# One DMA for the load of x and one for each tile's store, inverse stage 2 in half groups over two PSUM buffers, and layer norms sooner, in a long-convolution and MLP kernel

## The chip, the cores and the metric

The kernel runs on one core of one Trainium2 chip. The metric is the device time of one execution in microseconds (us), as the median of several executions; the kernel before took 240.22 us (three executions, 240.03 to 240.64). "Profile" and "trace" mean one execution recorded by the hardware profiler; its span is some 2 us shorter than the time (238.6 against 240.35 in the profiled execution), so spans are compared with spans and times with times. An execution counts as slow when it took over 1.5% more than the fastest of its kernel. Medians and ranges below are over all executions, slow ones too; ratios are of fast executions alone, and so are the profiles unless said otherwise.

In the views PE is TensorE (matmuls), DVE is VectorE, ACT is ScalarE, POOL is GpSimd, and SP is the engine that issues most DMAs; PSUM is the memory that matmuls write. The tiles: `pz` is what inverse stage 2 leaves in PSUM and `zt` its copy; `qln` and `hln` are the two layer norms, `pt` and `hlnT` the transposed `hln`; `ps1m` and `ps2m` are the two MLP layers' products, and `o` is a finished tile. The "granted clock" is the share of TensorE's full clock that it was given.

## The reference, cut to what matters

```python
# B, S, D, Dff = 1, 2048, 512, 1376; all inputs bfloat16
x  = A_q
q  = layernorm(x)
kv = shift_conv(A_k, A_shift_k) * A_v
y  = irfft(rfft(pad(kv)) * rfft(pad(A_ssm_k)))[:S] + kv * A_ssm_D   # long convolution over S
h  = x + q * y
out = h + relu(layernorm(h) @ B_w1) @ B_w2
```

The kernel computes the convolution as a Fourier transform in two stages of matmuls each way. The change is in what follows: the last inverse stage ("inverse stage 2"), the two layer norms and the start of the MLP.

## The kernel before

The 2048 tokens are 16 row tiles of 128 rows, in four groups of four tiles. `xh` holds x for all tiles, later h. A tile's token order is permuted: partition 32a + b of tile t holds token 64b + 16a + t, so a tile is four pieces of 32 rows in DRAM.

```python
def _tokens(src2d, t0, nt):            # four access patterns of 32 rows each
    D = src2d.shape[1]
    return [bass.AP(tensor=src2d.tensor, offset=src2d.offset + (16 * a + t0) * D, ap=[[64 * D, 32], [1, nt * D]])
            for a in range(4)]
# ...
for a, src in enumerate(_tokens(x_d, 0, NT)):
    nc.sync.dma_start(out=xh[32 * a:32 * a + 32, :, :].rearrange("p t d -> p (t d)"), in_=src)
# ... loads of w1 and w2 on the same queue
pzp = pl.push("psZ", bufs=1, space=PSUM)      # 4 banks, one buffer
ptp = pl.push("psT", bufs=1, space=PSUM)      # 1 bank, for the transposes
psum = pl.push("psM", bufs=3, space=PSUM)     # 3 banks, for the MLP

def inv2(q):                                  # inverse stage 2 of a group: small fp32 matmuls
    pz = pzp.tile([P, 4, 4, P], F32, tag="pz", name="pz")
    # ... 32 matmuls of 32x32 by 128 columns for each tile (two records each in a trace)
    return pz

def inv2_copy(q, pz):                         # four ACT copies pz -> zt, one for a tile
    # ...

def chain(q):                                 # groups 1 to 3: off the critical path, transposed by DMA
    qln = ln1(q)                              # layer norm of x
    hln = new_rows(q)
    gate(q, four(q), qln, hln)                # h = x + qln * z, then the layer norm of h
    # ... dma_start_transpose hln -> hlnT

# in mlp2(sc), for each tile: o = ps2 + xh, then
for a, dst in enumerate(_tokens(out_d, t, 1)):
    nc.sync.dma_start(out=dst, in_=o[32 * a:32 * a + 32, :])

# the schedule
qln = ln1(0, on_act=True)
inv2_copy(0, inv2(0))
hln = new_rows(0)
gate(0, [0, 1], qln, hln, on_act=True)
gate(0, [2, 3], qln, hln, on_act=True)
pz = inv2(1)
transposes(0, hln)                            # 8 TensorE transposes and one ACT copy to hlnT
mlp1(0, slice(0, 2 * P))                      # MLP layer 1 for the first two tiles
transposes(2, hln)
inv2_copy(1, pz)
mlp1(0, slice(2 * P, 4 * P))
chain(1)
inv2_copy(2, inv2(2))
mlp2(0)
chain(2)
mlp1(1)
# ... inv2(3), mlp2(1), chain(3), then mlp1 and mlp2 of groups 2 and 3
```

## Time and profile before

| what | before, us | from |
|---|---|---|
| time | 240.22 | median of 3 |
| span of the profile | 238.6 | profile |
| xh's DMAs issued from | 107.25 | timeline |
| DVE first reads xh | 124.19 | timeline |
| first matmul of inverse stage 2 | 124.99 | chain |
| first MLP matmul | 141.08 | chain |
| first matmul of inverse stage 2 of group 2 | 154.90 | timeline |
| last residual add (o) done | 234.77 | timeline |

The rows are the milestones used below. The views themselves stand in the prediction. In a chain each line is the start, the length, and what the end of the kernel hung on in that stretch.

### The profile page before, as it was taken

What the parts mean: (1) busy time and instruction counts of PE and PEld (TensorE: products, weight loads), DVE (VectorE), ACT (ScalarE), POOL (GpSimd) and SP (SyncE); (2) the same over time, 40 slices, a digit from 0 to 9 for tenths busy, and PEclk for the clock granted to TensorE, in tenths of its full rate; (3) what the DMA queues carried; (4) which work ended last, traced back from release to release, by engine and by line L of the source; (5) the groups of instructions that cost most, each with busy time, mean ns of one, the idle gap of its engine ahead of it and who ended that gap; (6) DMA issues with size and microseconds to landing.
All of it is one profiled execution on the core that took longest, in us unless ns stands there. A gap on an engine that the chain in (4) does not pass through costs nothing.

```text
span 238.6 us, 7218 instructions
## 1 busy us (share of the span) xinstructions
PE 206.1 (86%) x3100; PEld 145.8 (61%) x3100; DVE 154.2 (65%) x299; ACT 130.7 (55%) x241; POOL 62.7 (26%) x88
## 2 busy tenths in 40 slices
PE   0486998999767999998989678899999999979992
PEld 0473555999646999978986546764446444434440
DVE  7886986877655989977995882822577257740031
ACT  3779464666775688897992338912262327105500
POOL 6399700000003999975000001020022002200000
PEclk9999999999955899999999779999999999999998
DMA  6999910000000000009992000023200420042011
GB/s 212 286 206 157 190 34 4 3 1 0 3 5 3 3 1 0 3 1 201 195 368 70 3 3 0 3 46 69 61 8 3 93 71 17 0 91 65 23 44 44
DMA packets 30191, 15.45 MB, mean 65 GB/s; under 512 B 25584, under 2 KB 29008, under 8 KB 30032
## 3 DMA queue, kind: packets, MB, share of 16 engines
q1 hardware_dynamic: 29088, 14.93, 28.3%
q8 instruction: 24, 0.39, 0.7%
q10 hardware_dynamic: 1072, 0.07, 0.4%
q14 instruction: 7, 0.06, 0.1%
HBM read 7.08 MB, written 2.10 MB: 38 GB/s over the span
## 4 chain that ended last, share of the span: by engine, by line
PE 79%; ACT 9%; DMA 5%; DVE 4%; issue 2%; SPq 0%; ACTq 0%
PE ps1m L486 16%; PE ps2m L496 15%; PE pz L417 9%; PE psi L389 6%; PE pst L196 5%; PE psy L326 5%; PE pkv L254 5%; PE u L226 4%; PE u L228 4%; DMA sk<-in_A_ssm_k_dram 4%; PE ps L212 3%; PE ps2k L226 3%; PE ps2k L228 3%; ACT zt L425 2%; ACT c2c L174 2%
## 5 line engine op out<-in xcount | busy, mean ns | idle before, releaser
L488 ACT ACTIVATE h1T<-ps1m 128x512 bf16<-128x512 f32 (+3 forms) x55 | 28.0, 515 | 39.3 <-PE ps1m L486 38.5
L486 PE MATMUL ps1m<-hlnT,w 128*128 128x512 bf16 (+3 forms) x220 | 40.5, 346 | 4.5 <-ACT hlnT L508 2.2
L496 PE MATMUL ps2m<-w,h1T 128*128 128x512 bf16 (+1 forms) x176 | 38.7, 379 | 0.0
L486 PEld LDWEIGHTS <-w 128*128 128x128 bf16 (+1 forms) x220 | 22.6, 103 | 22.1 <-issue 5.3
L499 DVE TENSOR_TENSOR o<-ps2m,xh 128x512 bf16<-128x512 f32 x16 | 11.0, 691 | 38.2 <-PE ps2m L496 38.2
L316 DVE TENSOR_TENSOR t<-u,kf 128x704 fp32r<-128x704 f32 x32 | 27.1, 889 | 4.8 <-ACT usb L312 4.8
L496 PEld LDWEIGHTS <-h1T 128*128 128x128 bf16 (+1 forms) x176 | 17.0, 98 | 21.1 <-issue 0.8
L316 POOL TENSOR_TENSOR t<-usb,kf 128x320 fp32r<-128x320 f32 x32 | 28.7, 924 | 3.4 <-ACT usb L312 2.3
L417 PE MATMUL pz<-bp,ecore 32*32 32x128 f32 x1024 | 22.1, 387 | 4.2 <-ACT zt L425 2.2
L434 POOL TENSOR_SCALAR rstd<-mv 128x4 f32<-128x4 f32 x6 | 1.4, 229 | 88.5 <-DVE mv L441 88.5
L417 PEld LDWEIGHTS pz<-bp,ecore 32*32 32x32 f32 x1024 | 15.8, 108 | 9.8 <-issue 2.9
L439 DVE BATCH_NORM_STATS2 st<-xh 128x6 f32<-128x512 bf16 x32 | 19.8, 680 | 0.0
L328 ACT CAST kf<-psy 128x512 fp32r<-128x512 f32 x32 | 18.4, 645 | 1.6
L389 PE MATMUL psi<-dre,kf 128*128 128x256 f32 x64 | 15.8, 288 | 0.9 <-ACT kf L328 0.9
L425 ACT CAST zt<-pz 128x512 bf16<-128x512 f32 x16 | 8.2, 602 | 13.9 <-PE pz L417 13.9
L326 PE MATMUL psy<-t,ipos 128*128 128x512 f32 x48 | 15.8, 390 | 0.0
L389 PE MATMUL psi<-dim,kf 128*128 128x256 f32 x64 | 15.4, 283 | 0.0
L254 PE MATMUL pkv<-kT,wdiag 128*128 128x512 bf16 x64 | 15.2, 381 | 0.0
L196 PE MATMUL pst<-ident,sk 128*128 128x128 bf16 x64 | 6.7, 299 | 9.2 <-DMA sk<-in_A_ssm_k_dram 9.2
L201 ACT CAST a1k<-ps 128x512 fp32r<-128x512 f32 x20 | 10.4, 593 | 6.7 <-PE ps L212 6.7
L283 DVE TENSOR_TENSOR kf<-ps2k,dtab 128x512 fp32r<-128x512 f32 x16 | 11.0, 694 | 3.5 <-PE ps2k L228 3.4
L284 ACT CAST kf<-ps2k 128x512 fp32r<-128x512 f32 x16 | 10.2, 641 | 5.5 <-PE ps2k L228 5.3
(108 smaller groups left out, 410.0 us busy)
## 6 DMA issues: line engine op xcount, KB each, us to landing
sk<-in_A_ssm_k_dram SPq DMA_DIRECT2D x1, 2048.0 KB, 8.4
xh<-in_A_q_dram SPq DMA_DIRECT2D x4, 512.0 KB, 8.6
out_dram<-o SPq DMA_DIRECT2D x64, 32.0 KB, 1.6
w<-in_B_w_dram SPq DMA_DIRECT2D x1, 1376.0 KB, 15.1
w<-in_B_w_dram SPq DMA_DIRECT2D x1, 1280.0 KB, 18.2
hlnT<-hln SPq DMA_TRANSPOSE x12, 2.5
w<-in_B_w_dram SPq DMA_DIRECT2D x1, 96.0 KB, 17.8
dtab<-in_A_ssm_D_dram ACTq DMA_DIRECT2D x2, 32.0 KB, 8.4
```

Source lines behind the costliest of these rows:

```text
L196: nc.tensor.transpose(out=pst[:, i, :], in_=src[:, :, :, 8 * q + i], identity=ident[:])
L226: nc.tensor.matmul(out=ps[:, kk, :], lhsT=w_re[:, k1, :], rhs=a_in[:, k1, :], start=True, stop=False, skip_group_check=True)
L254: nc.tensor.matmul(out=ps[:], lhsT=wdiag[:, rg, j, :], rhs=kT[c][:, rg, 16 - j:CH + 16 - j], start=(j == 0), stop=(j == KS - 1))
L316: eng.tensor_tensor(out=t[:, :, j, :], in0=in0.unsqueeze(1).to_broadcast([P, 2, n, 2]), in1=kfr[:, :, j, ks], op=ALU.mult)
L326: nc.tensor.matmul(out=psy[:], lhsT=m_[:], rhs=t_.rearrange("p j k -> p (j k)"), start=first, stop=not first)
L328: nc.scalar.copy(out=kf[:, s, :, 2 * kp:2 * kp + 2], in_=psy[:].rearrange("p (j k) -> p j k", k=2))
L389: nc.tensor.matmul(out=ps[:, i, :], lhsT=kf[:, c, 4 * m:4 * m + 4, :].rearrange("p r k -> p (r k)"), rhs=d[:].rearrange("p a b -> p (a b)" ...
L417: nc.tensor.matmul(out=pz[32 * a:32 * a + 32, r4, l4, :], lhsT=ecore[rows, rho, n2, :], rhs=rhs, start=(rho == 0), stop=(rho == 1), tile_p ...
L439: nc.vector.bn_stats(out=st[:, t % 4, :], in_=xh[:, t, :])
L486: nc.tensor.matmul(out=ps1[:fsz, :], lhsT=w1[:, c, fc * P:fc * P + fsz], rhs=hlnTs[sc][:, c, part], start=(c == 0), stop=(c == DC - 1))
L488: nc.scalar.activation(out=h1s[sc][:fsz, fc, part], in_=ps1[:fsz, :], func=ACT.Relu)
L496: nc.tensor.matmul(out=ps2[:], lhsT=h1s[sc][:ksz, fc, i * P:(i + 1) * P], rhs=w2[:ksz, fc, :], start=(fc == 0), stop=(fc == NFC - 1))
```

## The change

The intent has four parts. Two PSUM buffers of four banks each, of which each half of a group takes one, so that group 1 of inverse stage 2 needn't wait for all of group 0's copies (half groups). The second eight transposes midway through the first MLP pass (midway transposes). The first layer norm of groups 2 and 3 ahead of the MLP layer that precedes them on DVE (layer norms sooner). And one DMA for four (xh's load and each tile's store).

```diff
 def _tokens(src2d, t0, nt):
-    return [bass.AP(..., offset=src2d.offset + (16 * a + t0) * D, ap=[[64 * D, 32], [1, nt * D]])
-            for a in range(4)]
+    return bass.AP(..., offset=src2d.offset + t0 * D, ap=[[16 * D, 4], [64 * D, 32], [1, nt * D]])
@@ load of xh
-    for a, src in enumerate(_tokens(x_d, 0, NT)):
-        nc.sync.dma_start(out=xh[32 * a:32 * a + 32, :, :].rearrange("p t d -> p (t d)"), in_=src)
+    nc.sync.dma_start(out=xh[:].rearrange("p t d -> p (t d)"), in_=_tokens(x_d, 0, NT))
@@ pools
-    pzp = pl.push("psZ", bufs=1, space=PSUM)
-    ptp = pl.push("psT", bufs=1, space=PSUM)
-    psum = pl.push("psM", bufs=3, space=PSUM)
+    pzp = pl.push("psZ0", bufs=2, space=PSUM)
@@ store of a tile
-            for a, dst in enumerate(_tokens(out_d, t, 1)):
-                nc.sync.dma_start(out=dst, in_=o[32 * a:32 * a + 32, :])
+            nc.sync.dma_start(out=_tokens(out_d, t, 1), in_=o[:])
@@ schedule
-    inv2_copy(0, inv2(0))
     hln = new_rows(0)
-    gate(0, [0, 1], qln, hln, on_act=True)
-    gate(0, [2, 3], qln, hln, on_act=True)
-    pz = inv2(1)
+    for ts in ([0, 1], [2, 3]):
+        inv2_copy(0, ts)                      # inv2 of half a group, then its two copies
+        gate(0, ts, qln, hln, on_act=True)
+    for ts in ([0, 1], [2, 3]):
+        inv2_copy(1, ts)
+    pl.pop("psZ0")
+    ptp = pl.push("psT", bufs=1, space=PSUM)
+    psum = pl.push("psM", bufs=3, space=PSUM)
+    pzp = pl.push("psZ", bufs=1, space=PSUM)
     transposes(0, hln)
-    mlp1(0, slice(0, 2 * P))
-    transposes(2, hln)
-    inv2_copy(1, pz)
+    mlp1(0, slice(0, 2 * P), lambda: transposes(2, hln))
     mlp1(0, slice(2 * P, 4 * P))
-    chain(1)
-    inv2_copy(2, inv2(2))
+    chain(1, ln1(1))
+    inv2_copy(2)
+    qln = ln1(2)
     mlp2(0)
-    chain(2)
+    chain(2, qln)
 # ... group 3 likewise
```

More of the change, by code (lines that the diff above doesn't have):

```diff
@@ L51, in _tokens @@
     D = src2d.shape[1]
-    return [bass.AP(tensor=src2d.tensor, offset=src2d.offset + (16 * a + t0) * D, ap=[[64 * D, 32], [1, nt * D]])
-            for a in range(4)]
+    return bass.AP(tensor=src2d.tensor, offset=src2d.offset + t0 * D, ap=[[16 * D, 4], [64 * D, 32], [1, nt * D]])
 @with_exitstack
@@ L406, with inv2 @@
     zts, hlnTs, h1s = {}, {}, {}
-    def inv2(q):
+    def inv2(q, l4s=(0, 1, 2, 3)):
         pz = pzp.tile([P, 4, 4, P], F32, tag="pz", name="pz")
-        for l4 in range(4):
+        for l4 in l4s:
             for rho in range(2):
@@ L420, in inv2, with inv2_copy @@
         return pz
-    def inv2_copy(q, pz):
-        zts[q] = hp.tile([P, 4, D], BF16, tag="zt", name="zt")
-        for l4 in range(4):
+    def inv2_copy(q, l4s=(0, 1, 2, 3)):
+        pz = inv2(q, l4s)
+        if q not in zts:
+            zts[q] = hp.tile([P, 4, D], BF16, tag="zt", name="zt")
+        for l4 in l4s:
             nc.scalar.copy(out=zts[q][:, l4, :].rearrange("p (m r) -> p m r", r=4),
@@ L469, in new_rows, with chain @@
         return ep.tile([P, 4, D], BF16, tag="hln", name="hln")
-    def chain(q):
-        qln = ln1(q)
+    def chain(q, qln):
         hln = new_rows(q)
@@ L476, in chain, with mlp1 @@
             nc.sync.dma_start_transpose(out=hlnTs[q][:, :, i * P:(i + 1) * P], in_=hln[:, i, :])
-    def mlp1(sc, part=slice(0, 512)):
+    def mlp1(sc, part=slice(0, 512), midway=None):
         if sc not in h1s:
@@ L482, in mlp1 @@
         for fc in range(NFC):
+            if fc == NFC // 2 and midway is not None:
+                midway()
             fsz = min(P, DFF - fc * P)
@@ L510 @@
     qln = ln1(0, on_act=True)
-    inv2_copy(0, inv2(0))
     hln = new_rows(0)
-    gate(0, [0, 1], qln, hln, on_act=True)
-    gate(0, [2, 3], qln, hln, on_act=True)
-    pz = inv2(1)
+    for ts in ([0, 1], [2, 3]):
[7 more added lines that the diff above has]
+    pzp = pl.push("psZ", bufs=1, space=PSUM)
     transposes(0, hln)
-    mlp1(0, slice(0, 2 * P))
-    transposes(2, hln)
-    inv2_copy(1, pz)
+    mlp1(0, slice(0, 2 * P), lambda: transposes(2, hln))
     mlp1(0, slice(2 * P, 4 * P))
-    chain(1)
-    inv2_copy(2, inv2(2))
+    chain(1, ln1(1))
+    inv2_copy(2)
+    qln = ln1(2)
     mlp2(0)
-    chain(2)
+    chain(2, qln)
     mlp1(1)
-    inv2_copy(3, inv2(3))
+    inv2_copy(3)
+    qln = ln1(3)
     mlp2(1)
-    chain(3)
+    chain(3, qln)
     for sc in (2, 3):
```

## The prediction

In it, k is the number of DMA engines that one DMA uses. Engines are out of step when a piece of 16 KB takes them 0.629 us, the fastest of the kernel before, and in step when it takes 1.28 us, the steady state there.

> **What bounds the kernel now.** I read the busy shares first, then the chain of work that ended last, then the timeline from 117 us, the waits of TensorE and the DMA table.
>
> ```profile
> PE 206.1 (86%) x3100; PEld 145.8 (61%) x3100; DVE 154.2 (65%) x299; ACT 130.7 (55%) x241; POOL 62.7 (26%) x88
> ...
> PEclk9999999999955899999999779999999999999998
> ```
>
> TensorE is busy 86% of the span and carries 79% of the chain. The second row is its granted clock in slices of 6 us; the dip to 7 lies at 131 to 143 us, in the part that the change rebuilds. Everything before 124 us is untouched. From there the chain reads (start, length, what):
>
> ```profile
> 124.99 4.42 PE pz L417 x188
> 129.41 0.51 issue
> 129.92 1.31 PE pz L417 x44
> 131.31 2.06 ACT zt L425 x4
> 133.42 4.58 PE pz L417 x188
> ...
> 139.43 0.57 PE pt L507 x8
> 140.02 1.02 ACT hlnT L508
> 141.08 6.44 PE ps1m L486 x44
> 147.52 0.46 PE pt L507 x8
> 148.00 1.01 ACT hlnT L508
> 149.01 1.96 ACT zt L425 x4
> 150.97 0.30 ACT h1T L488
> 151.31 3.65 PE ps1m L486 x32
> ...
> 211.04 0.70 DVE o L499
> 211.75 0.45 SPq L476
> 212.29 2.45 DMA hlnT<-hln
> ```
>
> The reader sees the places where the chain leaves TensorE: the four zt copies at 131.31 (one pz buffer of four PSUM banks, so group 1 waits for group 0's copies), the two hlnT copies, the zt copies at 149.01 that sit in ACT's queue ahead of the Relu copies, and the last hln transposes. TensorE's own waits there are 2.20 us at 131.2, 1.10 at 140, 1.10 at 148, 0.78 at 150.5 and 1.49 at 213.4. The rest after 154.90 is matmul upon matmul (the chain has stretches of 9.5 to 9.7 us of one MLP stage each), which the change doesn't touch.
>
> The last view is the DMA table (KB of each, us from issue to landing), with the first reader of xh in the timeline:
>
> ```profile
> sk<-in_A_ssm_k_dram SPq DMA_DIRECT2D x1, 2048.0 KB, 8.4
> xh<-in_A_q_dram SPq DMA_DIRECT2D x4, 512.0 KB, 8.6
> out_dram<-o SPq DMA_DIRECT2D x64, 32.0 KB, 1.6
> ```
>
> ```profile
> 124.19 2.46 DVE L439 BATCH_NORM_STATS2 st<-xh 128x6 f32<-128x512 bf16 x4
> ```
>
> xh is issued from 107.25; its fourth part is issued at 108.6 and lands 11.5 later, at 120.1. DVE first reads it at 124.19, so today there are 4.1 us of slack and nobody waits for it.
>
> [...] Before, a part has 32 rows on both sides: k = 16. Afterwards the DRAM side is [4, 32, row], and the built program carries it so, beside 128 partitions: k = 4. No DMA of the kernel before has such a shape, so its trace can't confirm it. [...] in the transfer records a 16 KB piece of xh took 0.629 us at its fastest (26 GB/s) but 1.28 us in the steady state, where 16 engines write 32 partitions; all of xh moved in 10.9 us, 192 GB/s. [...] the clock was 0.50 at 134 to 136 us and at 142 to 144, after the gaps at 131 and 140. [...]
>
> **The change part by part, first with xh in time.**
>
> *Half groups.* A half is 64 of 128 matmuls, about 2.7 us at the rate of 124.99 to 129.41. Group 0 ends at 131.2 as now, but its first half is out at 127.7, is copied (two copies of 0.51) by 128.8, and the gate of the first two tiles starts when qln is ready, 128.98 (now 131.93). Group 1 follows without the 2.20 us wait and ends near 137.2 instead of 139.4. The gate takes 4.3 us a half as now (first qln product 131.93 to last hln 136.22), so the second hln half is done near 137.5 (now 140.3). But ACT runs in order: the copies of group 1 stand behind the square root of the second gate half (136.5), and the transposes' bank is one of group 1's, free at 137.5. Then 0.57 transposes, 1.0 hlnT copy behind the last zt copies (138.6): the first MLP matmul starts at 139.7 instead of 141.08, 1.4 us sooner.
>
> *Midway transposes.* The second 8 transposes run between matmuls and their copy beside them. Gone: 1.10 + 0.78. The 88 matmuls of 128x256 took 0.146 us each in the first pass (half of it at the low clock) and 0.1195 in the second; if the low-clock stretches go, another 1.2. From 139.7: 88 x 0.1195 + 0.5 = 11.0, plus 0 to 1.5 for a low clock, ends at 150.7 to 152.2 (now 154.90). Gain 2.7 to 4.2, including the 1.4.
>
> *Layer norms sooner.* ln1 of group 3 (2.46 + 0.36 + 1.5 POOL + 1.38 = 5.7 us) moves ahead of mlp2(1), so its gate starts at about 195.1 instead of 200.5, and the transposes end 5 us sooner. The wait of 1.49 goes. The other groups have slack of over 5 us: 0.
>
> *One DMA for a tile.* SP issues 4 x 0.42 us now; the last of the kernel starts at 236.1, 1.3 after o is done (234.77). With 16 engines this would save about 0.9. With 4, each engine has 32 rows of 1 KB at 0.048 us (the trace's median) = 1.5 us[...]: 0.4 to 1.9 lost.
>
> Sum with xh in time: -2.7 to -4.2, -1.5, and at the end -0.9 to +1.5: about -5, 235 us.
>
> **The xh load.** With k = 4 each engine moves 32 rows of 16 KB. Estimate from the trace's durations: first piece 1.8 us after issue, at 109.0; 32 x 0.629 = 20.1 us, landing at 129; [...] 32 x 1.28 = 41 us, landing at 150. Call the landing L. From L: stats to qln 4.8 us (124.19 to 128.98 now), the first gate half to L + 9.1, second to L + 13.5, because it needs zt copies that stand behind the first square root on ACT; group 1's copies follow the second root, L + 14.5; hlnT copy L + 15.5; MLP from L + 15.6, 12.5 us with one cold window, ends at L + 28.1. Against 154.90 that is L - 126.8: +2.7 us for L = 129.5, +23 for 150. Taking off 1.5 for the last chain and adding about 1 at the end: +2 (242) or +22 (262). In the early case the half groups just pay for the late xh. w1 and w2 queue behind xh on those engines, but by 4 x 8 x 0.113 = 3.6 us and some 4 more only, before their readers.
>
> **Rivals.**
> - k is 16 after all (the lowering reshapes the pattern): [...] xh at least as early as now, and the gain of 5 us stands: 233.5 to 235.5. For it: sk, 128 rows in one DMA, moves 2 MB in 8.4 us. [...]
> - k = 4, the engines drift out of step: 242. For: some first pieces of xh in the records started 0.4 to 0.7 us after the others. [...]
> - k = 4 in step: 262. [...] Against: whoever wrote the change would have seen so large a loss, if it was timed.
> - The MLP's PSUM buffers bind (ACT's 1.0 us copy midway delays three buffers of 0.59 each): at most 0.5 us.
> - A lower clock eats the gain: 1.5 us.
>
> **Range and chances.** I give the in-time case 0.3 (its gain of 2.0 to 2.8% straddles the line, two thirds of it over 2%), 242 a weight of 0.35 and the slow case with what lies between 0.35. The middle of that is 243; eight in ten lie within 234 to 263. Faster by over 2%: 0.20; within: 0.43; slower: 0.37.
>
> **What would show it.** xh's single DMA: landing 20 us or 40 us after issue says k = 4, 6 to 11 says 16. If late, DVE's first stats start after 124.2 with a wait on the DMA, and ACT's zt copies wait for the square root. The pz group 1 should begin at once after group 0 if xh is in time. The chain should show no zt copies at 149, no DMA hlnT at 212. out DMAs should land in 2.5 us or more if k = 4. I am wrong altogether if xh lands late and the time still falls, or if it lands early and the time doesn't.

## The result, and the profile after

The changed kernel took 263.79 us (median of four, 263.21 to 263.98), the kernel before 240.43 us in the same rounds (240.03 to 243.92). The ratio is 1.0974, 95% interval 1.0946 to 1.1002: slower by 9.7%. A ratio here is the mean time of one kernel's fast runs over that of the other's of the same rounds, so it is not quite the ratio of the medians quoted.

First the page of the changed kernel, TensorE's row of busy times and the granted clock in 40 slices (of 6.5 us here):

```profile
PE 206.3 (79%) x3085; PEld 147.3 (56%) x3100; DVE 154.1 (59%) x299; ACT 130.6 (50%) x241; POOL 62.4 (24%) x88
...
PEclk9999999999657999999995555599999999999997
```

TensorE's work is the same, 206.3 us against 206.1, in a span 23 us longer. The five slices at 5, from 137 to 170 us, cover most of the time in which it stood still, and its first work after that. Next the chain of waits of the same kernel:

```profile
109.25 40.51 DMA xh<-in_A_q_dram
...
149.78 2.47 DVE st L437 x4
...
161.41 0.29 ACT rstd L429
161.70 1.94 ACT zt L423 x4
...
163.69 1.02 PE pt L505 x8
...
165.85 4.42 PE ps1m L485 x20
```

The end of the kernel now hangs on the load of x for 40.5 us. From its landing at 149.75 the first gate runs, half by half, then group 1's copies (zt), the transposes (pt) and the MLP (ps1m) at 165.85, where before the MLP began at 141.08. DVE's first read of xh in the timeline carries the wait itself (start, length, and in brackets the idle time and its releaser):

```profile
149.78 2.47 DVE L437 BATCH_NORM_STATS2 st<-xh 128x6 f32<-128x512 bf16 x4 [23.49 <-DMA xh<-in_A_q_dram]
```

and the DMA table has one issue for each load and store:

```profile
xh<-in_A_q_dram SPq DMA_DIRECT2D x1, 2048.0 KB
out_dram<-o SPq DMA_DIRECT2D x16, 128.0 KB
```

Beneath these views lie the records of single transfers. The DMAs end with records of 4 bytes, read here as one for each engine that a DMA used. There were 1841 such records before and 821 after. Taking away 64 stores and 4 loads of 16 each and adding 17 DMAs of 4 each gives 1841 - 1088 + 68 = 821. Four transfers of 16 KB for xh were under way at once for 33.9 of its 38.5 us, where 16 were for 7.8 of 10.9 us before. And of the pieces of w1 and w2, which are issued behind xh, just a quarter (128 of 512 and 344 of 1376) started only from 147.4 us on; the last of them ended at 156.6. So the single load used four engines of 16. The 128 pieces of 16 KB that make up xh took 1.22 us each in the median, 0.608 at the fastest, and ran for 38.5 us together.

| distance, us | before | after |
|---|---|---|
| issue of xh to landing | 12.9 to the last part (107.25 to 120.1) | 40.5 |
| xh needed or landed to first MLP matmul | 16.9 (124.19 to 141.08) | 16.1 |
| first MLP matmul to group 2's inverse stage 2 | 13.8 | 12.6 |
| from there to the end of the span | 83.7 | 83.5 |

So the whole loss is the load. What the other three parts gave is only some 2 us in this table, and the question is whether the rest was hidden behind the late load or never there.

### The profile page after: what moved, and what is told of

Same layout as the page of the kernel before. It is cut to its first block, busy times and chain, and to the rows that moved or that the text cites. A ratio compares the mean times of both kernels' runs of the same rounds, so it can differ in the third digit from the quotient of the medians.

```text
span 261.9 us, 7138 instructions
## 1 busy us (share of the span) xinstructions
PE 206.3 (79%) x3085; PEld 147.3 (56%) x3100; DVE 154.1 (59%) x299; ACT 130.6 (50%) x241; POOL 62.4 (24%) x88
## 4 chain that ended last, share of the span: by engine, by line
PE 64%; DMA 19%; DVE 7%; ACT 5%; issue 3%; POOLq 0%; DVEq 0%; ACTq 0%
DMA xh<-in_A_q_dram 15%; PE ps1m L485 15%; PE ps2m L495 15%; PE psy L325 6%; PE pst L195 5%; PE pkv L253 4%; PE pz L413 4%; PE u L225 4%; PE u L227 3%; DMA sk<-in_A_ssm_k_dram 3%; PE ps L211 3%; PE ps2k L227 3%; PE ps2k L225 3%; DVE st L437 2%; ACT c2c L173 2%
## 5 line engine op out<-in xcount | busy, mean ns | idle before, releaser
L495 PE MATMUL ps2m<-w,h1T 128*128 128x512 bf16 (+1 forms) x172 | 38.5, 379 | 0.2
L429 ACT ACTIVATE rstd<-mv,eps_t 128x2 f32<-128x2 f32 (+1 forms) x3 | 0.9, 296 | 30.7 <-DVE mv L439 30.7
L387 PE MATMUL psi<-dim,kf 128*128 128x256 f32 x64 | 15.4, 283 | 0.0
L200 ACT CAST a1k<-ps 128x512 fp32r<-128x512 f32 x20 | 10.4, 594 | 8.3 <-PE ps L211 8.3
L387 PEld LDWEIGHTS psi<-dre,kf 128*128 128x128 f32 x64 | 12.2, 191 | 1.6 <-ACT kf L327 1.3
```

The costliest lines, as they stand in the source:

```text
L387: nc.tensor.matmul(out=ps[:, i, :], lhsT=kf[:, c, 4 * m:4 * m + 4, :].rearrange("p r k -> p (r k)"), rhs=d[:].rearrange("p a b -> p (a b)" ...
L495: nc.tensor.matmul(out=ps2[:], lhsT=h1s[sc][:ksz, fc, i * P:(i + 1) * P], rhs=w2[:ksz, fc, :], start=(fc == 0), stop=(fc == NFC - 1))
```

## The experiments

Eleven runs of ten kernels, all correct. The first four undo or isolate the DMAs.

### xh4: the changed kernel with xh loaded in four DMAs again

```diff
-    nc.sync.dma_start(out=xh[:].rearrange("p t d -> p (t d)"), in_=_tokens(x_d, 0, NT))
+    for a, src in enumerate(_tokens4(x_d, 0, NT)):      # the old four patterns
+        nc.sync.dma_start(out=xh[32 * a:32 * a + 32, :, :].rearrange("p t d -> p (t d)"), in_=src)
```

> The changed kernel with the row load xh in its four old DMAs again (k = 16 engines each); half groups, sooner layer norms and the single store of each tile stay. Theory A (the single xh load on 4 engines is the whole loss, 40.5 us from issue to landing in the changed kernel): xh lands at about 120, DVE's first stats start right after its bp copies without a wait on a DMA, and the rest of the change shows its gain: 234.5 to 237, with about 1 us lost at the end by the single store. Rival B (half groups or the order on ACT lose time by themselves): the stats start in time and the kernel still takes over 243.

Measured: 239.22 us (238.89 to 241.97), before 240.21 (238.79 to 243.08), ratio 0.9977 [0.9931, 1.0023]: the same as before. DVE's first read of xh in the timeline has no wait any more:

```profile
125.85 2.46 DVE L445 BATCH_NORM_STATS2 st<-xh 128x6 f32<-128x512 bf16 x4
```

One load undone takes back the whole loss. It also shows that the other parts, with xh in time, gain hardly anything.

### before_xh1: the kernel before with xh alone in one DMA

```diff
+    nc.sync.dma_start(out=xh[:].rearrange("p t d -> p (t d)"), in_=_tokens1(x_d, 0, NT))   # in place of the four
```

> The kernel before with only the xh load made one DMA. Theory A: 4 completions for it in the transfer records, landing 40 us after issue, DVE waits for it by some 24 us; in the kernel before the chain from landing to the first MLP matmul is longer or as long (124.19 to 141.08 is 16.9 us), so 262 to 266, at least the loss of the whole change. Rival B: below 255.

Measured: 260.37 us (259.38 to 262.01), ratio 1.0852 [1.0792, 1.0912]. Two lines of its chain:

```profile
107.69 40.11 DMA xh<-in_A_q_dram
...
160.69 6.63 PE ps1m L491 x44
```

The load alone costs 8.5% in the old kernel too. It landed at 147.8 and the MLP began 12.9 us later, while the changed kernel needed 16.1. With a late xh the half groups thus make the path 3.2 us longer: there the copies of group 1 and, behind them, the transposes follow the square root of the second gate half (161.41 in the chain shown above), whereas here the transposes ran right behind group 1's matmuls, at 158.8, and only the hlnT copy followed that square root (159.45). The 260.37 lies below the 262 to 266 expected: the expectation took the old order's path from landing to MLP to be as long as the new one's or longer, and it was shorter.

### before_out1: the kernel before with each tile stored in one DMA

```diff
-            for a, dst in enumerate(_tokens(out_d, t, 1)):
-                nc.sync.dma_start(out=dst, in_=o[32 * a:32 * a + 32, :])
+            nc.sync.dma_start(out=_tokens1(out_d, t, 1), in_=o[:])
```

> The kernel before with only the stores made one DMA for each tile. Theory A: each shows 4 completions and lands later than a quarter did, the time from the last o to the end goes from 3.8 to about 4.9 us and nothing else waits for a store: +0.5 to +1.5 us (240.7 to 241.9). Rival C: -0.5 or less.

Measured: 241.22 us (240.15 to 244.15), ratio 1.0036 [0.9996, 1.0075]. From the end of the last o to the end of the span it took 4.24 us, against 3.83 before. Four engines lose about as much in the transfer as three fewer issues of 0.42 us save, and 0.4 us more in this trace; in the time it isn't shown, as the interval includes no change.

### both4: xh and the stores in four DMAs, the rest of the change kept

```diff
 # xh4, and in mlp2:
-            nc.sync.dma_start(out=_tokens(out_d, t, 1), in_=o[:])
+            for a, dst in enumerate(_tokens4(out_d, t, 1)):
+                nc.sync.dma_start(out=dst, in_=o[32 * a:32 * a + 32, :])
```

> As xh4, and the stores of the tiles also in four DMAs of 32 rows. Theory A: the last store costs 3.8 us from the last o to the end as in the kernel before (the changed kernel 4.86), so 0.7 to 1.2 us faster than xh4: 233.5 to 236. Rival C (one issue for four saves more than 4 engines lose): slower than xh4 by 0.5 or more.

Measured: 239.24 us (237.28 to 239.88), ratio 0.9946 [0.9903, 0.9988]. So half groups, midway transposes and layer norms gain 1.3 us together (0.3 to 2.3), where I had put -5 with the stores at about zero. The expectation of 233.5 to 236 failed too, and beside xh4 the median is the same (239.22), so the time doesn't show what the stores cost. Its chain from the start of inverse stage 2 to the MLP shows why:

```profile
124.49 4.42 PE pz L421 x188
128.91 0.20 issue
129.11 2.75 PE pz L421 x115
131.86 0.54 issue
132.40 2.76 PE pz L421 x113
135.16 1.08 issue
136.24 1.33 PE pz L421 x45
...
137.60 1.08 ACT zt L431 x2
...
138.72 0.62 PE pt L514 x8
...
139.42 1.02 ACT hlnT L515
...
140.48 4.42 PE ps1m L493 x20
```

The wait of 2.20 us on the zt copies is gone, as intended. In its place stand three pauses called issue, 1.82 us in all: time in which TensorE waited for nothing that the profile shows (before, 0.63 us of these were in the same stage). And the transposes now wait for the last zt copies, until 138.7. Both groups' tiles are buffers of one PSUM pool. My reading was that closing that pool waits for both, so that the first transpose waits for the very last copy and not for those of the buffer whose bank it takes over; psplit below tests this. The old kernel could transpose as soon as the matmuls were done (139.43) and copied zt afterwards (149.01). The stage of the matmuls fell by 1.4 us (14.44 to 13.08) and the stretch from its end to the MLP grew by 1.3 (1.65 to 2.91).

### pair01 and pair12: two engines, on partitions 0 to 63 or on 32 to 95

Two quarters of xh are loaded as before with 16 engines each, the other two in one DMA of two blocks, whose slowest dimension is 2. In pair01 those are partitions 0 to 63, in pair12 partitions 32 to 95. The bytes, the number of engines and the pattern are the same. The partitions differ, and with them the rows of DRAM that are read (16 KB apart between the two engines in both) and the two quarters that are loaded beside.

```diff
-    nc.sync.dma_start(out=xh[:].rearrange("p t d -> p (t d)"), in_=_tokens(x_d, 0, NT))
+    for a in (2, 3):                                    # pair12: (0, 3)
+        nc.sync.dma_start(out=xh[32 * a:32 * a + 32, :, :]..., in_=...ap=[[64 * D, 32], [1, NT * D]])
+    nc.sync.dma_start(out=xh[0:64, :, :]...,            # pair12: xh[32:96], offset + 16 * D
+                      in_=...ap=[[16 * D, 2], [64 * D, 32], [1, NT * D]])
```

> The changed kernel, but xh in three DMAs: parts 2 and 3 (partitions 64 to 127) as 32 rows each (k = 16), then parts 0 and 1 (partitions 0 to 63) as one DMA[...]: two engines of 32 pieces of 16 KB each[...]. Theory P[...]: some 1.2 us a piece, the pair takes about 38 us after the two quick parts (5 to 6 us), xh lands 44 to 48 us after its first issue, total 267 to 272. Rival E (an engine moves a piece of such a pattern in 1.2 us by itself, whatever its partner does): the same here.

> As pair01, but the pair is parts 1 and 2 (partitions 32 to 95): the same two engines, pieces and bytes[...]. Theory P: about 0.62 us a piece, the pair takes some 20 us, xh lands 26 to 30 us after its first issue, 16 to 20 us sooner than in pair01; total 249 to 254. Rival E: no difference between the two beyond 2 us.

Measured: pair01 263.7 us (260.6 to 265.46), ratio 1.0921 [1.0838, 1.1003]; pair12 252.13 us (251.12 to 252.36), ratio 1.0516 [1.0465, 1.0568]; before 239.85 in the same rounds. DVE's first read of xh in their timelines, pair01 first:

```profile
149.91 1.29 DVE L442 BATCH_NORM_STATS2 st<-xh 128x6 f32<-128x512 bf16 x2 [24.47 <-DMA xh<-in_A_q_dram]
```

```profile
138.45 2.47 DVE L442 BATCH_NORM_STATS2 st<-xh 128x6 f32<-128x512 bf16 x4 [14.08 <-DMA xh<-in_A_q_dram]
```

The bracket is the wait: 24.5 us and 14.1. Issue to landing was 40.5 us in pair01, as in the changed kernel with four engines, and 30.1 in pair12. Pair12's time met its expectation, and pair01's came in below its 267 to 272: counted from the first issue, xh landed after 41.4 us in pair01 (44 to 48 expected) and after 31.0 in pair12 (26 to 30), so that the gap between the two was 10.4 us and not 16 to 20. In the transfer records, once the other engines had written their shares of w1 and w2, a piece of 16 KB took 0.614 us in pair12 in the median (53 GB/s while both ran) and 1.20 in pair01 (30 GB/s). So the load is slow for two reasons that multiply: a single engine moves a piece in 0.61 us at best and has 32 of them (20 us), and two engines over partitions 0 to 63 mostly took twice as long for a piece (1.20 us in the median) as over 32 to 95 (0.614). What makes the two ranges differ isn't shown. That the cause lies on the side of the partitions, and not of the DRAM rows, is argued from the equal 16 KB distance and not tested apart. Pair12 didn't land after 20 us but after 30: until 123.8 us, some 15 after its first, most of its pieces, too, took about 1.2 us, and in that time the other two quarters and then the weights were being written. In pair01's records from 137 us on, of four pieces in a row of one engine two or so take 1.22, one 0.9 to 1.06 and one 0.62 to 0.67: one engine leads by about a piece, and one piece of four is about as fast as in pair12. Why it is one in four isn't shown.

### psplit: the two buffers in two pools

both4 with a pool of its own for each of the two buffers, so that the first half's four banks can be handed on when its own copies are done; nothing is moved.

```diff
-    pzp = pl.push("psZ0", bufs=2, space=PSUM)
+    pzb = pl.push("psZb", bufs=1, space=PSUM)           # second halves, later groups 2 and 3
+    pza = pl.push("psZa", bufs=1, space=PSUM)           # first halves
# ...
-    pl.pop("psZ0")
+    pl.pop("psZa")
```

> both4 with the two pz buffers in two pools of their own, so that the pool of the first halves can be closed without the second. Nothing else is moved. Theory W (closing the common pool makes the first transposes wait for the very last zt copy, about 1.1 us after the buffer they take is free): the first pt matmul starts right after the last pz matmul or after the third of the four zt copies of group 1, 0.5 to 1.1 us sooner against the start of pz than in both4 (14.2 us there); the MLP still waits for the hlnT copy behind the last zt copy in ACT's queue, so only 0.3 to 0.8 us in the total, which the noise may hide. Rival: pt waits for something else and starts as late as in both4.

Measured: 238.2 us (237.12 to 239.53), ratio 0.9928 [0.9871, 0.9986]. In the trace the transposes no longer wait for the last copies: they started at 140.81, before the matmuls' modelled end at 140.89, with no wait in front of them:

```profile
140.81 1.03 PE L517 MATMUL pt<-ident,hln 128*128 128x128 bf16 x8
```

But the hlnT copy still stands behind the zt copies in ACT's queue, so from the end of the matmuls to the MLP it took 2.11 us (both4: 2.91). The wait for the pool was real, worth 0.8 us in the trace; the times of both4 and psplit overlap.

### v1: copies ahead of the gate, transposes between the last matmuls

psplit, with the order changed so that neither ACT's queue nor the pool stands between the matmuls and the MLP.

```diff
-    for ts, pool in (([0, 1], pza), ([2, 3], pzb)):
-        inv2_copy(0, ts, pool)
-        gate(0, ts, qln, hln, on_act=True)
-    for ts, pool in (([0, 1], pza), ([2, 3], pzb)):
-        inv2_copy(1, ts, pool)
+    inv2_copy(0, [0, 1], pza)
+    gate(0, [0, 1], qln, hln, on_act=True)
+    inv2_copy(0, [2, 3], pzb)
+    inv2_copy(1, [0, 1], pza)                           # its copies ahead of the second gate's square root
+    gate(0, [2, 3], qln, hln, on_act=True)
     pl.pop("psZa")
# ... pools for transposes and MLP
+    pz = inv2(1, [2])                                   # third quarter of group 1
     transposes(0, hln)
+    inv2(1, [3], pz=pz)                                 # last quarter, beside the hlnT copy
+    inv2_copy(1, [2, 3], pz=pz)
```

> As psplit, and reordered: the zt copies of group 1's first half ahead of the second gate half (so before its square root on ACT), and the first transposes between the last two quarters of group 1's matmuls, their hlnT copy ahead of the last zt copies. Theory W: the first MLP matmul starts 12.5 to 14 us after the start of pz (16.0 in both4), 2 to 3.5 us off the total against both4: 234.5 to 237.5. Rival I ([...] issue gaps of 0.2 to 1.1 us between groups): the pz matmuls take longer as soon as waits go, and under 1 us is gained.

Measured: 233.84 us (232.98 to 235.17), ratio 0.9769 [0.9725, 0.9813]: faster than both kernels, though the interval leaves open whether by 2%. Its chain at that place, and the clock row of its page:

```profile
133.72 0.81 issue
134.52 2.54 PE pz L423 x98
137.06 0.55 PE pt L517 x8
137.61 1.87 PE pz L423 x63
139.49 1.42 PE ps1m L496 x12
```

```profile
PEclk9998899999975699999999999999999999999998
```

TensorE goes from the matmuls into the MLP without a stop. From the first pz matmul to the first MLP matmul it took 13.1 us (before 16.1, both4 16.0), and the first MLP layer of group 0 took 10.6 us (13.8 and 12.9). That is twice 44 matmuls of 0.12 us: in this trace the low clock at 131 to 143 us is gone. This is the gain that the half groups were meant to bring.

### ln_only: the kernel before with the layer norms sooner, nothing else

```diff
-    chain(1)
+    chain(1, ln1(1))
     inv2_copy(2, inv2(2))
+    qln = ln1(2)
     mlp2(0)
-    chain(2)
+    chain(2, qln)
 # ... group 3 likewise
```

> The kernel before with one part of the change alone: the layer norms of groups 2 and 3 stand ahead of the second MLP layer of the group before. Theory (this part works as predicted): the chain no longer has the last hlnT transfer and o + issue in front of it at 211 us, and from the first inverse stage 2 matmul of group 2 to the end it takes 82.2 us instead of 83.7; the time falls by 1.5 us, 238.7 us, ratio 0.994. Rival (those 1.6 us of the changed kernels come from the half groups, which shift everything behind): 83.7 us stay and the ratio is 1.000.

Measured: 238.8 us (237.77 to 241.18), before 241.43 (238.42 to 243.87, a noisy chip), ratio 0.9978 [0.9895, 1.0061]: the time alone decides nothing. The trace does. The end of its chain is matmuls upon matmuls, with none of the lines o, issue and DMA hlnT that stood at 211 us:

```profile
203.74 9.51 PE ps2m L495 x44
213.25 9.50 PE ps1m L485 x44
222.75 9.53 PE ps2m L495 x44
```

From group 2's inverse stage 2 to the end it took 82.21 us, against 83.4 to 83.8 in the three traces of kernels of the old order. So this part is worth 1.5 us by itself. One more thing is in this trace: the first 44 MLP matmuls took 4.96 us, where the same 44 in the same order took 6.44 before, without a change there. What differed was the granted clock, 1.00 over these 44 against 0.76.

### v1b and v2: the gain again, and the last stores on two queues

v1b is v1 unchanged. v2 is v1 with

```diff
-                nc.sync.dma_start(out=dst, in_=o[32 * a:32 * a + 32, :])
+                (nc.scalar if t == NT - 1 and a % 2 else nc.sync).dma_start(out=dst, in_=o[32 * a:32 * a + 32, :])
```

> A second timing of v1, unchanged, on another chip or another day: 233.8 us and a ratio of 0.977, between 0.972 and 0.982, if its gain is real; above 0.985 if the first timing was luck.

> v1 with the last tile's four stores issued in turn by SP and ACT. In the kernels with four stores the fourth issue begins 1.3 us after the last o is done, because each issue takes 0.42 us on SP. Theory (the last issue sets the end): last o to end falls from 3.8 to about 3.0 us, the time by 0.8 us beside v1b, ratio 0.973. Rival (a store's own transfer and its completion set the end, or ACT's issue is slower): within 0.3 us of v1b.

Measured: v1b 235.8 us (233.18 to 236.93), ratio 0.9794 [0.9715, 0.9874]; v2 234.12 us (232.31 to 236.22), ratio 0.9728 [0.9647, 0.9808]. v1's gain is there again, within the range expected, though the interval again reaches past 2%. The trace is less good than v1's: from the first pz matmul to the first MLP matmul it took 14.1 us and not 13.1, with a pause of 1.08 us and one stretch of low clock (136.8 to 140.2) before the MLP; the first MLP layer again took 10.6. v2's profiled run was slow, but only its end is read. Its timeline has the two ACT issues just behind the last o, which ended at 231.18:

```profile
231.22 0.85 ACTq L511 DMA_DIRECT2D out_dram<-o  x2
```

From the last o to the end it took 3.12 us, against 3.77 in v1b: 0.65 us gone, near the 0.8 expected. The times agree in sign, but their intervals overlap, so the gain in time isn't shown.

## Why the prediction was wrong

**The load's number of engines was right, its size too.** Four engines in step were the third branch of the prediction. Its terms against the trace:

| term | predicted | measured |
|---|---|---|
| issue of xh | 107.25 | 109.25 |
| landing | 150 | 149.75 |
| landing to first MLP matmul | 15.6 | 16.1 |
| first MLP matmul to group 2's inverse stage 2 | 12.5 | 12.57 |
| inverse stage 2 of group 2 starts at | 178.1 | 178.42 |
| from there to the end | 83.7 - 1.5 + 1 = 83.2 | 83.5 |

The trace has four completion records for the load. The doubled time of a piece is what pair01 and pair12 differ in, 1.20 us and 0.614. The 2 us of later issue were made up by a slightly faster transfer (40.5 us from issue to landing, where 42.8 were put).

**The step that failed is the choice between the two costs of a piece in "The xh load", and the weights and the range in "Range and chances" that were built on it.** The prediction worked out both costs, 0.629 us a piece for engines out of step (242 us) and 1.28 for engines in step (262), and gave the second, which came true, only 0.35, so that its middle was 243. The runs showed 1.22 us a piece in the median and 40.5 us from issue to landing. It also rounded its own sum down: L - 126.8 = 23.2, less 1.5, plus 1, is 22.7, so 262.9 and not the 262 that the text carried on with. A range that ends at 263 leaves nothing above its worst branch. The result was 263.79, from 0.3 us more up to 178.42, 0.3 more behind it, and the rest from the time beside the span and the spread between executions. As for the weight: for the engines drifting apart spoke first pieces that started 0.4 to 0.7 us late; but the records of pair01 show a lead of about a piece that lasts, while only one piece of four is about as fast as in pair12 (0.62 to 0.67 us). The other argument, that whoever wrote the change would have seen so large a loss, was about people and not in any view. The one duration measured through a whole load of xh, 1.28 us a piece in the median, should have carried most of the weight.

**The gain with xh in time was mis-sized.** The text said about -5; both4 measured -1.3 (by its trace -2.6 from the first pz matmul to the end: 113.6 to 111.0). By terms:

- *Half groups*, "the first MLP matmul starts at 139.7 ... 1.4 us sooner": both4 has 16.0 us from the first pz matmul, before 16.1, so 0.1 and not 1.4. Two things failed. The matmuls were to end after 12.2 us and took 13.08, because issue pauses filled the place of the wait. And "the transposes' bank is one of group 1's, free at 137.5" overlooked that both buffers belong to one pool: with the pools apart the distance fell to 15.4 (psplit), and with the copies and transposes reordered to 13.1 (v1).
- *Midway transposes*, 2.7 to 4.2 less 1.4, so 1.3 to 2.8: the first MLP layer of group 0 took 12.9 us in both4, 11.9 in xh4 and 12.5 in psplit against 13.8 to 14.0 in three traces of the old order. The gain is 0.9 to 2.1, but how much of it is this part isn't shown, since ln_only took 12.3 without it, at another clock. The low clock, "if the low-clock stretches go", stayed until v1.
- *Layer norms sooner*, -1.5: right, 83.7 to 82.2 in ln_only.
- *One DMA for a tile*, 0.4 to 1.9 lost by the author's estimate: right at its lower end, 0.4 in before_out1 and in xh4 and 1.0 in the changed kernel (4.86 from the last o to the end, 3.83 before). The sum, though, put -0.9 to +1.5 for it, and its -0.9 holds only for 16 engines.

**What sets off the low clock is open.** The prediction puts the clock of 0.50 after the gaps at 131 and 140. These were 2.20 and 1.10 us long. Each low stretch of this stage lasted 3.4 us (133.9 to 137.3 and 140.7 to 144.1), and the 3.4 us ahead of it held 2.2 and 0.9 us in which TensorE stood still. The 3.4 us from 147.6 held 1.5 us, and the clock stayed full (1.00). So the halving is measured, but what sets it off isn't.

**"Everything before 124 us is untouched"** holds for the program, not for the times: over the traces the first pz matmul came between 124.5 and 127.6 us in the fast ones, in kernels of either order. That is as large as the parts that were being weighed, and why they are measured here as distances.

**What stays open.** What TensorE does in the issue pauses of 0.2 to 1.1 us between pz matmuls isn't shown; no experiment took them away. The kept traces hold a lead, though: transfers of 16 KB on a queue that the page of a profile calls "instruction". In the thirteen traces all 35 pauses of over 0.15 us between pz matmuls for which no other wait is seen ended 1.2 to 1.6 us after such a transfer had landed (1.4, 1.2 and 1.4 us for the three of both4). The page lists 24 of them. In the kernel before one landed at 132.4 us, in the middle of the wait on the zt copies. That the pauses wait for these transfers isn't shown: no run tests it. And between both4's -1.3 us in time and -2.6 in its trace I can't decide, with one trace and so much spread between executions; the profiled one was the fastest of its six (237.28).

## What to carry to other kernels

When several DMAs are joined into one, count in a trace how many engines it uses: saving three issues of 0.4 us cost 28 us of landing time here, because the engines fell from 16 to 4 (completion records a DMA) and each piece took 1.22 us in the median, where the fastest took 0.608. When a wait is removed, look for what stands directly behind it (here a shared pool, then the copies ahead in ACT's queue), because the gain comes only when the last of them goes. And when a prediction splits into branches, take the weights from measured durations, and let the range reach past the worst branch by the run-to-run spread.
